# Long and short matmuls in turn: the two products of an MLP step, and the two parts of a token mix

## The chip, the cores and the metric

One core of a Trainium2 chip. The time is that of the device, in microseconds; the kernel before took 563.84 us in the median of three runs (562.71 to 564.00).

## The reference

Three stages on two batches of 768 tokens with 512 channels, all in fp32:

```
scores = q @ k.T / 8 - slope * distance;  keep: 96 positions back, and the first 8
x  = softmax(scores) @ v                                   # 8 heads of 64
xn = (x - mean(x)) / sqrt(var(x) + 1e-6) * g_ln
x  = x + relu(xn @ w_ch1) @ w_ch2                          # first mix: 512 -> 2048 -> 512
theta = x @ w_theta                                        # second mix
y  = W_r @ (x * cos(theta)) + W_i @ (x * sin(theta))       # token mix: 768 x 768, per batch
u  = x + y
out = u + relu(u @ w_ch)
```

## The kernel before

TensorE multiplies in fp32r, so every operand is split into a high and a low part, and every product is three matmuls: high x high, high x low, low x high.

**First mix.** The 12 tiles of 128 tokens are taken in 6 chunks of two tiles. The 2048 hidden channels are 16 blocks of 128, in four rounds of four blocks. A round has 24 steps, one for each chunk and block. A step computes, in `mlp_h`, the hidden block of a chunk, hp (128 hidden channels x 256 tokens): 12 matmuls of 256 columns (line 403). ScalarE takes the relu of it as hh (line 409), VectorE the rest as hl (line 410). In `mlp_o` hh and hl of an earlier step are the stationary operands and the rows of w_ch2 the moving ones: 6 matmuls of 512 columns into the two op tiles of the chunk (line 429). After the four blocks of a round op is scaled by the token's 1/std and added to x (`add_mix`, line 417).

What the names stand for: hh and hl are kept in three buffers each, in a pool where each buffer begins 64 bytes past a multiple of 512 in a partition's row. The banks of PSUM are handed out by tag: two "h" (hp), two "o", two "s", one "pt" and one "m". In rounds 2 and 3 every third hp goes to "m", so hp has three banks there, and in round 4 two.

**Order.** Round 1 runs beside the attention. The rounds 2 to 4 are the loop at lines 902 to 925: in each step first the 12 hp, then, where round 4's `early` has some, a piece of the second mix's start, then the 6 op of the step two before (of the step before, at the start of round 2 and in round 4), then the split of the weights that this freed (`split_w`, lines 362 to 372) and the decoding of the next ones (`decode`, lines 343 to 353; the weights arrive as packed words). A scheduler orders the instructions of each engine by their place in the program and their readiness in its own model; matmuls stand in the program's order but for small shifts.

**Second mix.** For each tile theta is 12 matmuls of 512 columns (thm, line 517); ScalarE and VectorE make cos and sin (`sincos`, lines 523 to 532) and the products with x (`rotate`, lines 536 and 537). The token mix (`tok`, line 606) takes one tile of 128 source tokens in a step, 12 steps in all, six for each batch: `tok_part` multiplies the channels of that tile (stationary) by the rows of W_r and W_i (moving). Part 0 gives target tokens 0 to 511 in four tiles of 512 columns, part 1 gives tokens 512 to 767 in four half tiles of 256; 24 matmuls each (line 582). They add up over a batch's six steps in six banks, taken as acc from the tags h, h, s, s, o, o; acc4 and acc5 hold part 1. In the batch's last step `add_y` (line 597) adds each acc to x on VectorE, and its bank is free. Behind it `last` multiplies by w_ch (ch, line 628) and writes the output.

```
banks = [ps(tag, [P, DM], f"acc{b}_{n}") for n, tag in enumerate(("h", "h", "s", "s", "o", "o"))]
for part in range(2):
    for d in range(KD):
        tok_part(b, s, d, part)
```

Of the kernel before, what the change touches and what calls it, by code (L numbers as in the profile page):

```python
# [1 line left out]

# [6 lines left out]
F32 = mybir.dt.float32  # L9
# [21 lines left out]
NE = 4  # L31
NPT = 2

PAD = 32


@with_exitstack
def kernel(ctx, tc, q, kwin, v, n_pair, g_ln, wall, out):
# [53 lines left out]
        nc.vector.scalar_tensor_tensor(nval, words[:, :, 1], 2.0**32, low, ALU.mult, ALU.add)  # L92

    def test_n():
        fast = act.tile([P, 6], F32, tag="bn", name="fast", bufs=2)
        nc.vector.tensor_scalar(fast[:, 0:1], nval[:, 0:1], 0.0, None, ALU.is_ge)
        nc.vector.tensor_scalar(fast[:, 1:2], nval[:, 0:1], float(GLOB), None, ALU.is_le)
        nc.vector.tensor_scalar(fast[:, 2:3], nval[:, 1:2], 1.0, None, ALU.is_ge)
        nc.vector.tensor_scalar(fast[:, 3:4], nval[:, 1:2], float(PREV), None, ALU.is_le)
        nc.vector.tensor_tensor(fast[:, 0:2], fast[:, 0:2], fast[:, 2:4], ALU.mult)  # L100
        nc.vector.tensor_tensor(fast[:, 0:1], fast[:, 0:1], fast[:, 1:2], ALU.mult)
        nc.vector.tensor_scalar(slow, fast[:, 0:1], -1.0, 1.0, ALU.mult, ALU.add)
# [252 lines left out]
    def decode_to(n):  # L355
        for i in range(len(piece), min(n, 2 * NF)):
            piece[i] = w_pool.tile([P, DM], F32, tag="w", name=f"w{i}", bufs=NW)
            decode(i, piece[i])
# [32 lines left out]
    def mlp_h(c, f, tag, part=None):  # L391
        cn = len(CHUNKS[c]) * P
        xh, xl = xt_t[c]
        wh, wl = split_t[f][0:2]
        if part != 1:
            hp_t[c, f] = ps(tag, [P, cn], f"hp{c}_{f}")
        hp = hp_t[c, f]
        kks = range(KD) if part is None else range(part * KD // 2, (part + 1) * KD // 2)
        n = 3 * kks[0]
        for kk in kks:  # L400
            a, al = wh[:, kk * P:(kk + 1) * P], wl[:, kk * P:(kk + 1) * P]
            for l, r in ((a, xh), (a, xl), (al, xh)):
                nc.tensor.matmul(hp, l, r[:, kk, :], start=(n == 0), stop=(n == 3 * KD - 1))  # L403
                n += 1
        if part == 0:
            return
        hh = act.tile([P, cn], F32R, tag="hh", name=f"hh{c}_{f}", bufs=3)
        hl = act.tile([P, cn], F32R, tag="hl", name=f"hl{c}_{f}", bufs=3)
        nc.scalar.activation(hh, hp, AF.Relu)  # L409
        nc.vector.scalar_tensor_tensor(hl, hp, 0.0, hh.bitcast(F32), ALU.max, ALU.subtract)  # L410
        ht_t[c, f] = (hh, hl)
# [7 lines left out]
    def mlp_o(c, f, fs, js=(0, 1)):  # L419
        if f == fs[0] and 0 in js:  # L420
            tags = ("s",) * 2 if c % 2 and f >= GROUP else ("o",) * 2
            op_t[c] = [ps(tags[j], [P, DM], f"op{c}_{f}_{t}") for j, t in enumerate(CHUNKS[c])]
        hh, hl = ht_t[c, f]
        wh, wl = split_t[f][2:4]
        for j in js:
            t = CHUNKS[c][j]
            a, al = hh[:, j * P:(j + 1) * P], hl[:, j * P:(j + 1) * P]
            for n, (l, r) in enumerate(((a, wh), (a, wl), (al, wh))):
                nc.tensor.matmul(op_t[c][j], l, r, start=(f == fs[0] and n == 0), stop=(f == fs[-1] and n == 2))  # L429
            if f == fs[-1]:  # L430
                add_mix(t, op_t[c][j])
                if f == NF - 1:
                    ready.add(t)

# [134 lines left out]
    def tok_part(b, s, d, part):  # L571

        w, z = toks[b, s], z_t[b * NQ + s]
        o = acc[b][part][d]
        dsl = slice(d * P, (d + 1) * P)
        for n, (zh, zl) in enumerate(z):
            wh, wl = w[1] if part else w[2 * n]
            sl = slice(n * SB, (n + 1) * SB) if part else slice(0, SA)
            for m, (l, r) in enumerate(((zh, wh), (zh, wl), (zl, wh))):
                first, end = s == 0 and n == 0 and m == 0, s == NQ - 1 and n == 1 and m == 2  # L580
                paired = part == 1
                mm = nc.tensor.matmul(  # L582
                    o, l[:, dsl], r[:, sl], start=first and not (paired and d % 2), stop=end and not (paired and d % 2 == 0)
                )
                if paired and (first or end):
                    tc.keep_in_program_order(mm)

    def x_cols(b, d, part):
        t0, t1 = (SA // P, NQ) if part else (0, SA // P)
# [16 lines left out]
    def tok(b, s):  # L606
        if s == 0:
            banks = [ps(tag, [P, DM], f"acc{b}_{n}") for n, tag in enumerate(("h", "h", "s", "s", "o", "o"))]
            acc[b] = (banks[0:KD], [banks[KD + d // 2][:, d % 2 * SB:(d % 2 + 1) * SB] for d in range(KD)])
        for part in range(2):  # L610
            for d in range(KD):
                tok_part(b, s, d, part)
                if s == NQ - 1:
                    for d_ in [d] if part == 0 else [d - 1, d] if d % 2 else []:
                        add_y(b, d_, part)
# [216 lines left out]

    def down(j, js):
        c, f = items[j]
        mlp_o(c, f, GROUPS[0], js)
        if js[-1] and c == NCH - 1 and f + GROUP < NF:
            split_w(f + GROUP)

# [2 lines left out]
    with tc.manual_schedule(engines=ENGINES):  # L841
        for k in range(LEAD + len(items) + 1):
            j = k - LEAD
            u = k - 1
            mix = 0 <= j < len(items)
            xp_of = HEAD + (k - 3) // U if k % U == 1 and 0 <= (k - 3) // U < NTT - HEAD else None
            xt_of = HEAD + (k - 4) // U if k % U == 0 and 0 <= (k - 4) // U < NTT - HEAD else None
            if k == 0:
                flip_probs(*blocks[1], 2, True)
                values(*blocks[1], 1)  # L850
                flip_probs(*blocks[1], 3, True)
                spin("o", "idle0", 5)
            if k == 1:
                values(*blocks[1], 2)
                values(*blocks[1], 3)
                lift_x(*blocks[1])
            if 0 <= u < NU:
                flip_probs(*unit(u)[:2], unit(u)[2][0], False)
            if k < NU:
                b, i, ps_ = unit(k)  # L860
                if k % U == 0:
                    loads_to(HEAD + k // U + 2)
                scores(b, i, ps_, False)
            if k == 1:
                make_xt(SEQ[0])
                finish_x(*blocks[1], True)
                layer_norm(SEQ[1])
            if k == 2:
                make_xt(SEQ[1])
            if mix:  # L870
                mlp_h(*items[j], "h", 0)
            elif 0 < k < LEAD:
                spin("o", f"idle{k}", 5)
            if 0 <= u < NU:
                flip_probs(*unit(u)[:2], unit(u)[2][1], False)
            if mix:
                mlp_h(*items[j], "h", 1)
            if xt_of is not None:
                make_xt(SEQ[xt_of])
            if 0 <= j - 1 < len(items):  # L880
                down(j - 1, [0])
            if xp_of is not None:
                finish_x(*blocks[xp_of], False)
            if 0 <= j - 1 < len(items):
                down(j - 1, [1])
            if 0 < k < LEAD:
                spin("o", f"wait{k}", 5)
            if 0 <= u < NU:
                for p in unit(u)[2]:
                    values(*unit(u)[:2], p)  # L890
                if u % U == U - 1:
                    lift_x(*unit(u)[:2])
            if xp_of is not None:
                layer_norm(SEQ[xp_of])
            if 0 <= k < 2 * GROUP - 2:
                with behind_exp(len(maxima) - 1):
                    split_w((k + 2) // 2, ((k + 2) % 2,))
            elif k >= 7:
                with behind_maximum(min(len(maxima) - 1, 16 + 4 * k + 3)):
                    decode_to(2 * GROUP + min(NW, (k - 5) // 2))  # L900
# [3 lines left out]
    for n, (g, c, f) in enumerate(work):  # L904
# [6 lines left out]
        if n == (NR - 2) * ROUND + 2 * NW + 1:  # L911
            early = early_steps()
        middle = ROUND + 2 <= n < (NR - 1) * ROUND
        mlp_h(c, f, "m" if middle and n % 3 == 0 else "h")
        next(early, None)
        while done[0] < n - (1 if middle else 0):
            pg, pc, pf = work[done[0]]
            mlp_o(pc, pf, GROUPS[pg])
            if pc == NCH - 1 and pf + GROUP < NF:
                split_w(pf + GROUP)  # L920
            done[0] += 1
        decode_to(2 * GROUP * (rnd + 1) + min(NW, n % ROUND // 2))
    for _ in early:
        pass
    mlp_o(*work[-1][1:], GROUPS[-1])

    act_es.close()
    ws_es.close()
# [90 lines left out]
```

## Time and profile before

| what | value |
|---|---|
| median of three runs | 563.84 us (562.71 to 564.00) |
| profiled execution | 563.2 us |
| its span | 561.4 us |
| TensorE busy | 546.8 us, 97% |
| VectorE, ScalarE, GpSimd busy | 359.8, 280.6, 103.4 us |
| share of PE in the chain that ended last | 66% |
| granted clock of TensorE, mean | 0.997 |

The span is the profiled stretch on the core; the execution's own time holds 1.8 us more around it. PE is TensorE's matmul, PEld its weight load, which overlaps it; DVE is VectorE, ACT ScalarE, POOL GpSimd. Matmuls follow one another in a pipeline, so the row of one shows a longer duration than the distance to the next one's start, and the distance is what it costs. [...]

### The profile page before, as it was taken

How to read it: one execution, taken by the hardware profiler on the slowest of the kernel's cores; microseconds unless marked ns; L12 is line 12 of the kernel's file. 1: busy time of each engine (PE TensorE's matmuls, PEld its weight loads, DVE VectorE, ACT ScalarE, POOL GpSimd, SP SyncE). 2: the span in 40 equal slices, each digit the busy share in tenths (PEclk: the TensorE clock that was granted, in tenths of full speed). 3: DMA queues.
4: the chain of work that ended last, by engine and by line, in shares of the span. 5: the costliest groups of instructions: out<-in, count | busy, mean ns of one | idle time of the engine just before them, and what ended most of it. 6: DMA issues, size and time to landing. Idle time of an engine off the chain costs nothing.

```text
span 561.4 us, 9278 instructions
## 1 busy us (share of the span) xinstructions
PE 546.8 (97%) x3554; PEld 461.9 (82%) x3557; DVE 359.8 (64%) x783; ACT 280.6 (50%) x647; POOL 103.4 (18%) x91
## 2 busy tenths in 40 slices
PE   8799999999998999999999999999999999999996
PEld 4367787787787999999889888889888888888895
DVE  6798787877757722298674424562699878870542
ACT  4677755555527411276562325561677777740110
POOL 1222100000013000030201102240033347730000
PEclk9999999999999999999999999999999999999998
DMA  8945544422013500045451000000234200000112
GB/s 260 338 157 188 195 148 142 133 76 74 13 67 112 188 1 1 0 151 189 149 188 39 0 1 1 0 2 2 104 122 147 78 2 0 2 1 1 75 72 85
DMA packets 18547, 49.17 MB, mean 88 GB/s; under 512 B 2240, under 2 KB 4288, under 8 KB 18496
## 3 DMA queue, kind: packets, MB, share of 16 engines
q1 hardware_dynamic: 18496, 48.51, 25.1%
q8 instruction: 30, 0.49, 0.3%
q14 instruction: 21, 0.17, 0.1%
HBM read 45.35 MB, written 3.15 MB: 86 GB/s over the span
## 4 chain that ended last, share of the span: by engine, by line
PE 66%; ACT 1%; DVE 1%; issue 0%; DVEq 0%; ACTq 0%
PE op L429 18%; PE hp L403 18%; PE acc L582 17%; PE thm L517 6%; PE ch L628 6%; PE xp L313 1%; DVE w L349 0%; ACT wt L343 0%; DVE hl L410 0%; ACT xth L314 0%; DVE dec L348 0%; ACT k L525 0%; ACT k L524 0%; ACT s L530 0%; ACT y L523 0%
## 5 line engine op out<-in xcount | busy, mean ns | idle before, releaser
L403 PE MATMUL hp<-xth,w1h 128*128 128x256 f32 x384 | 111.3, 290 | 0.0
L403 PE MATMUL hp<-xth,w1l 128*128 128x256 f32 x384 | 107.9, 281 | 0.0
L403 PE MATMUL hp<-xtl,w1h 128*128 128x256 f32 x384 | 107.8, 281 | 0.0
L410 DVE SCALAR_TENSOR_TENSOR hl<-hp,hh 128x256 fp32r<-128x256 f32 x96 | 40.3, 420 | 78.2 <-ACT hh L409 77.8
L403 PEld LDWEIGHTS hp<-xth,w1h 128*128 128x128 f32 x384 | 72.6, 189 | 9.2 <-issue 3.8
L582 PE MATMUL acc<-tokh,z 128*128 128x512 f32 (+1 forms) x320 | 79.2, 336 | 0.0
L429 PE MATMUL op<-w2h,hh 128*128 128x512 f32 x192 | 78.5, 409 | 0.0
L429 PE MATMUL op<-w2h,hl 128*128 128x512 f32 x192 | 76.4, 398 | 1.4 <-DVE hl L410 1.4
L429 PE MATMUL op<-w2l,hh 128*128 128x512 f32 x192 | 76.0, 396 | 0.0
L403 PEld LDWEIGHTS hp<-xtl,w1h 128*128 128x128 f32 x384 | 72.6, 189 | 3.7 <-DVE xtl L315 0.2
L409 ACT ACTIVATE hh<-hp 128x256 fp32r<-128x256 f32 x96 | 35.8, 374 | 74.4 <-PE hp L403 74.4
L403 PEld LDWEIGHTS hp<-xth,w1l 128*128 128x128 f32 x384 | 72.6, 189 | 0.1
L582 PEld LDWEIGHTS acc<-tokh,z 128*128 128x128 f32 x320 | 55.4, 190 | 6.6
L212 ACT ACTIVATE e<-e,nm 128x256 f32<-128x256 f32 (+1 forms) x96 | 46.0, 481 | 21.8 <-DVE nm L205 21.8
L582 PE MATMUL acc<-tokl,z 128*128 128x512 f32 (+1 forms) x160 | 53.8, 336 | 0.0
L371 POOL TENSOR_TENSOR w1l<-w,w1h 128x512 fp32r<-128x512 f32 x16 | 21.7, 1359 | 136.6 <-ACT w1h L370 136.6
L429 PEld LDWEIGHTS op<-w2h,hl 128*128 128x128 f32 x192 | 36.1, 188 | 12.6 <-DVE hl L410 4.0
L205 DVE CUSTOM_DVE_ANT_0 e<-s,bias 128x256 f32<-128x256 f32 (+1 forms) x96 | 33.5, 397 | 16.8 <-PE s L231 16.7
L544 POOL TENSOR_TENSOR x2all<-xth,xtl 128x512 f32<-128x512 f32 x12 | 18.3, 1527 | 121.1 <-DVE k L536 121.1
L494 DVE TENSOR_TENSOR tokl<-wt,tokh 128x512 fp32r<-128x512 f32 x36 | 34.0, 952 | 10.3 <-ACT tokh L493 10.1
L429 PEld LDWEIGHTS op<-w2h,hh 128*128 128x128 f32 x192 | 36.4, 190 | 4.3 <-ACT hh L409 0.4
L429 PEld LDWEIGHTS op<-w2l,hh 128*128 128x128 f32 x192 | 36.2, 188 | 3.8
(155 smaller groups left out, 1055.0 us busy)
## 6 DMA issues: line engine op xcount, KB each, us to landing
raw<-in_wall SPq DMA_DIRECT2D x58, 512.0 KB, 3.2
k<-in_kwin SPq DMA_DIRECT2D x10, 512.0 KB, 4.8
q<-in_q SPq DMA_DIRECT2D x12, 256.0 KB, 3.5
vc<-in_v SPq DMA_DIRECT2D x12, 256.0 KB, 3.4
out<-o SPq DMA_DIRECT2D x8, 256.0 KB, 2.0
vw<-in_v SPq DMA_DIRECT2D x10, 192.0 KB, 2.5
out<-o SPq DMA_DIRECT2D x8, 128.0 KB, 1.7
vw<-in_v SPq DMA_DIRECT2D x10, 64.0 KB, 3.6
```

Of the source, the lines that this page charges most:

```text
L205: r = nc.vector.tensor_tensor_reduce(out=e[:, j, :], in0=s[j], in1=bias[h][:, b0:b0 + nk], scale=-SCALE, scalar=3.0e38, op0=ALU.add, op1=A ...
L212: r = nc.scalar.activation(e[:, j, :], e[:, j, :], AF.Exp, bias=nm[:, h:h + 1], scale=-1.0, accum_out=sm[:, h:h + 1])
L371: (nc.vector if d and f >= GROUP else nc.gpsimd).tensor_tensor(lo, s, hi.bitcast(F32), ALU.subtract)
L403: nc.tensor.matmul(hp, l, r[:, kk, :], start=(n == 0), stop=(n == 3 * KD - 1))
L409: nc.scalar.activation(hh, hp, AF.Relu)
L410: nc.vector.scalar_tensor_tensor(hl, hp, 0.0, hh.bitcast(F32), ALU.max, ALU.subtract)
L429: nc.tensor.matmul(op_t[c][j], l, r, start=(f == fs[0] and n == 0), stop=(f == fs[-1] and n == 2))
L494: nc.vector.tensor_tensor(lo, src, hi.bitcast(F32), ALU.subtract)
L517: nc.tensor.matmul(mp, l[:, kk, :], r[:, kk, :], start=(n == 0), stop=(n == 3 * KD - 1))
L544: nc.gpsimd.tensor_tensor(x2[t], xh.rearrange("p k t -> p (k t)").bitcast(F32), xl.rearrange("p k t -> p (k t)").bitcast(F32), ALU.add)
L582: mm = nc.tensor.matmul(o, l[:, dsl], r[:, sl], start=first and not (paired and d % 2), stop=end and not (paired and d % 2 == 0))
L628: nc.tensor.matmul(mp, l[:, kk, es], r, start=(kk == 0 and m == 0), stop=(kk == KD - 1 and m == 2))
```

## The change

In rounds 2 to 4 `mlp_h` and `mlp_o` become generators, and a new function `run` draws from several of them in turn: two hp matmuls, one op matmul, six times a step. The op now belong to the step three before (two before in round 4), and the piece of `early` and the split of weights stand behind both. hh and hl have four buffers in place of three, and begin at multiples of 512 bytes, for which a small tile `fast` goes to another pool and a filler (PAD) shrinks from 32 to 24 words. In the token mix, in all but the last step of each batch, the matmuls of part 0 and part 1 alternate one by one. The number of matmuls, loads and vector instructions is the same. The added lines shift line numbers by 2 to 17: op stands at 432, hp at 405, hh and hl at 412 and 413, thm at 533, acc at 598, the add to x at 614.

```diff
-PAD = 32
+LAG = 3
+PAD = 24
...
-        fast = act.tile([P, 6], F32, tag="bn", name="fast", bufs=2)
+        fast = keep.tile([P, 6], F32, name="fast")
...
                 nc.tensor.matmul(hp, l, r[:, kk, :], start=(n == 0), stop=(n == 3 * KD - 1))
                 n += 1
+                yield
...
-        hh = act.tile([P, cn], F32R, tag="hh", name=f"hh{c}_{f}", bufs=3)
-        hl = act.tile([P, cn], F32R, tag="hl", name=f"hl{c}_{f}", bufs=3)
+        hh = act.tile([P, cn], F32R, tag="hh", name=f"hh{c}_{f}", bufs=4)
+        hl = act.tile([P, cn], F32R, tag="hl", name=f"hl{c}_{f}", bufs=4)
...
+    def run(*gens):
+
+        live = list(gens)
+        while live:
+            for g, n in list(live):
+                for _ in range(n):
+                    if next(g, live) is live:
+                        live.remove((g, n))
+                        break
...
+        if s < NQ - 1:
+            for d in range(KD):
+                run(*((tok_part(b, s, d, part), 1) for part in range(2)))
+            return
         for part in range(2):
             for d in range(KD):
-                tok_part(b, s, d, part)
+                run((tok_part(b, s, d, part), 1))
...
-        mlp_h(c, f, "m" if middle and n % 3 == 0 else "h")
+        steps = [(mlp_h(c, f, "m" if middle and n % 3 == 0 else "h"), 2)]
+        behind_ = []
+        while done[0] <= n - (LAG if n < (NR - 1) * ROUND else 2):
+            behind_.append(work[done[0]])
+            done[0] += 1
+        if behind_:
+            steps.append((chain(*(mlp_o(*x[1:], GROUPS[x[0]]) for x in behind_)), len(behind_)))
+        run(*steps)
         next(early, None)
-        while done[0] < n - (1 if middle else 0):
-            pg, pc, pf = work[done[0]]
-            mlp_o(pc, pf, GROUPS[pg])
-            if pc == NCH - 1 and pf + GROUP < NF:
-                split_w(pf + GROUP)
-            done[0] += 1
+        for x in behind_:
+            if x[1] == NCH - 1 and x[2] + GROUP < NF:
+                split_w(x[2] + GROUP)
```

On PE, in the first steps of round 2, the kernel before has the last hp of chunk 0, block 7, then the 6 op of block 5, then the hp of chunk 1 (the first numbers in a name are the chunk and the block):

```order
L403 MATMUL hp0_7_2411<-xtl0_480,w1h7_2331 128x256
L403 MATMUL hp0_7_2411<-xth0_479,w1l7_2332 128x256
L429 MATMUL op0_4_0_2378<-w2h5_2288,hh0_5_2374 128x512 [waits Activation_49]
L429 MATMUL op0_4_0_2378<-w2l5_2289,hh0_5_2374 128x512
L429 MATMUL op0_4_0_2378<-w2h5_2288,hl0_5_2375 128x512 [waits DVE_49]
L429 MATMUL op0_4_6_2379<-w2h5_2288,hh0_5_2374 128x512
L429 MATMUL op0_4_6_2379<-w2l5_2289,hh0_5_2374 128x512
L429 MATMUL op0_4_6_2379<-w2h5_2288,hl0_5_2375 128x512
L403 MATMUL hp1_4_2434<-xth1_768,w1h4_2253 128x256
L403 MATMUL hp1_4_2434<-xtl1_769,w1h4_2253 128x256
```

The same engine and place in the changed kernel, where the op of block 5 stand among the hp of chunk 1:

```order
L432 MATMUL op0_4_6_2407<-w2h4_2257,hl0_4_2358 128x512
L405 MATMUL hp1_4_2428<-xth1_768,w1h4_2253 128x256 [waits DVE_49]
L405 MATMUL hp1_4_2428<-xtl1_769,w1h4_2253 128x256
L432 MATMUL op0_4_0_2406<-w2h5_2288,hh0_5_2374 128x512 [waits Activation_49]
L405 MATMUL hp1_4_2428<-xth1_768,w1l4_2254 128x256
L405 MATMUL hp1_4_2428<-xth1_768,w1h4_2253 128x256
L432 MATMUL op0_4_0_2406<-w2l5_2289,hh0_5_2374 128x512
L405 MATMUL hp1_4_2428<-xtl1_769,w1h4_2253 128x256
L405 MATMUL hp1_4_2428<-xth1_768,w1l4_2254 128x256
L432 MATMUL op0_4_0_2406<-w2h5_2288,hl0_5_2375 128x512
```

The op have moved one step later, and the wait on VectorE now stands at the first hp of a step, for its bank.

On PE, at the first token-mix step of the second batch, the kernel before ends part 0 (acc1_3) before it begins part 1 (acc1_4):

```order
L582 MATMUL acc1_3_5394<-tokh1_0_0_5199,z0_6_4897 128x512 [waits DVE_49]
L582 MATMUL acc1_3_5394<-tokl1_0_0_5200,z0_6_4897 128x512
L582 MATMUL acc1_3_5394<-tokh1_0_0_5199,z0_6_4897 128x512
L582 MATMUL acc1_3_5394<-tokh1_0_2_5207,z1_6_4900 128x512
L582 MATMUL acc1_3_5394<-tokl1_0_2_5208,z1_6_4900 128x512
L582 MATMUL acc1_3_5394<-tokh1_0_2_5207,z1_6_4900 128x512
L582 MATMUL acc1_4_5395<-tokh1_0_1_5203,z0_6_4897 128x256 [waits DVE_49,PE_49]
L582 MATMUL acc1_4_5395<-tokl1_0_1_5204,z0_6_4897 128x256
```

In the changed kernel the same step begins, behind the last thm of tile 10, with:

```order
L533 MATMUL thm10_5357<-thh_3490,xtl10_5212 128x512
L598 MATMUL acc1_0_5391<-tokh1_0_0_5199,z0_6_4897 128x512 [waits DVE_49]
L598 MATMUL acc1_4_5395<-tokh1_0_1_5203,z0_6_4897 128x256 [waits DVE_49,PE_49]
L598 MATMUL acc1_0_5391<-tokl1_0_0_5200,z0_6_4897 128x512
L598 MATMUL acc1_4_5395<-tokl1_0_1_5204,z0_6_4897 128x256
L598 MATMUL acc1_0_5391<-tokh1_0_0_5199,z0_6_4897 128x512 [waits Pool_49]
L598 MATMUL acc1_4_5395<-tokh1_0_1_5203,z0_6_4897 128x256
```

The first matmul into acc1_4, with its wait on VectorE, has moved from the step's 25th place to its second. VectorE's own order there, which frees acc0_4, is the same in both kernels:

```order
L614 TENSOR_TENSOR x2all_70<-x2all_70,acc0_3_4670 128x4x128 [waits PE_49]
L614 TENSOR_TENSOR x2all_70<-x2all_70,acc0_4_4671 128x2x128 [waits PE_49]
L552 SCALAR_TENSOR_TENSOR k9_5233<-k9_5233,x2all_70 128x512 [waits Activation_49]
L614 TENSOR_TENSOR x2all_70<-x2all_70,acc0_4_4671 128x2x128
L614 TENSOR_TENSOR x2all_70<-x2all_70,acc0_5_4672 128x2x128 [waits PE_49]
L614 TENSOR_TENSOR x2all_70<-x2all_70,acc0_5_4672 128x2x128
```

Between the two halves of acc0_4 stands k, a product of the rotation of tile 9; nothing has moved.

## Rows read from the trace of the kernel before

**Rows 1.** The page: busy time by engine, and the chain's shares by line.
```profile
PE 546.8 (97%) x3554; PEld 461.9 (82%) x3557; DVE 359.8 (64%) x783; ACT 280.6 (50%) x647; POOL 103.4 (18%) x91
...
PE op L429 18%; PE hp L403 18%; PE acc L582 17%; PE thm L517 6%; PE ch L628 6%; PE xp L313 1%; DVE w L349 0%; ACT wt L343 0%; DVE hl L410 0%; ACT xth L314 0%; DVE dec L348 0%; ACT k L525 0%; ACT k L524 0%; ACT s L530 0%; ACT y L523 0%
```
**Rows 2.** The chain in order of time: start us, us, what.
```profile
180.15 2.87 PE hp L403 x24
...
208.43 1.42 PE hp L403 x12
209.85 1.40 PE op L429 x6
...
273.29 1.42 PE hp L403 x12
...
280.66 1.55 PE op L429 x6
...
337.84 1.42 PE hp L403 x12
...
444.70 2.75 PE thm L517 x12
447.45 8.31 PE acc L582 x48
```
**Rows 3.** PE's timeline behind a run of 256 columns: start us, us, what.
```profile
489.90 0.40 PE L582 MATMUL acc<-tokl,z 128*128 128x512 f32 x1
...
490.60 0.39 PE L582 MATMUL acc<-tokl,z 128*128 128x512 f32 x1
...
491.28 0.39 PE L582 MATMUL acc<-tokl,z 128*128 128x512 f32 x1
```
**Rows 4.** PE's timeline in the second batch's first token-mix step.
```profile
470.29 0.39 PE L582 MATMUL acc<-tokh,z 128*128 128x512 f32 x1
470.52 0.39 PE L582 MATMUL acc<-tokl,z 128*128 128x512 f32 x1
...
475.85 0.28 PE L582 MATMUL acc<-tokl,z 128*128 128x256 f32 x1
...
478.61 0.40 PE L517 MATMUL thm<-thh,xth 128*128 128x512 f32 x1
```
**Rows 5.** PE's timeline where the two sizes mix in round 4.
```profile
356.50 0.40 PE L517 MATMUL thm<-thl,xth 128*128 128x512 f32 x1
356.74 0.28 PE L403 MATMUL hp<-xth,w1l 128*128 128x256 f32 x1
356.85 0.28 PE L403 MATMUL hp<-xth,w1h 128*128 128x256 f32 x1
...
357.09 0.42 PE L517 MATMUL thm<-thh,xtl 128*128 128x512 f32 x1
```
**Rows 6.** VectorE's timeline beside the step of rows 4.
```profile
471.04 1.01 DVE L597 TENSOR_TENSOR x2all<-x2all,acc 128x512 f32<-128x512 f32 x2
471.99 1.38 DVE L536 SCALAR_TENSOR_TENSOR k<-k,x2all 128x512 f32<-128x512 f32 x1
473.29 1.07 DVE L597 TENSOR_TENSOR x2all<-x2all,acc 128x256 f32<-128x256 f32 x3
```
**Rows 7.** VectorE's timeline: hl at three places.
```profile
182.76 0.41 DVE L410 SCALAR_TENSOR_TENSOR hl<-hp,hh 128x256 fp32r<-128x256 f32 x1
...
280.54 0.42 DVE L410 SCALAR_TENSOR_TENSOR hl<-hp,hh 128x256 fp32r<-128x256 f32 x1
...
341.90 0.42 DVE L410 SCALAR_TENSOR_TENSOR hl<-hp,hh 128x256 fp32r<-128x256 f32 x1
```
**Rows 8.** Stretches at the end: us, busy by engine, granted clock, DMA share, GB/s.
```profile
556.50:558.50 2.00, 0.00 (x0) 0.00 (x0) 0.42 (x1) 0.00 (x0) 0.00 (x0) 1.00 0.35 118
558.50:559.50 1.00, 0.00 (x0) 0.00 (x0) 0.00 (x0) 0.00 (x0) 0.00 (x0) 0.54 0.09 25
```
**Rows 9.** PE's timeline at the program's start.
```profile
1.19 4.94 PE L77 MATMUL spin<-zero 128*128 128x512 bf16 x12 [1.19 <-DVE zero L119]
```

More of the change, by code (lines that the diff above doesn't have):

```diff
@@ L1 @@
 from contextlib import ExitStack
+from itertools import chain
 import concourse.bass as bass
@@ L429, in mlp_o @@
                 nc.tensor.matmul(op_t[c][j], l, r, start=(f == fs[0] and n == 0), stop=(f == fs[-1] and n == 2))
+                if n < 2:
+                    yield
             if f == fs[-1]:
@@ L433, in mlp_o @@
                     ready.add(t)
+            yield
+    def run(*gens):
[6 more added lines that the diff above has]
+                        break
     p2 = {}
@@ L586, in tok_part @@
                     tc.keep_in_program_order(mm)
+                yield
     def x_cols(b, d, part):
@@ L834, in down @@
         c, f = items[j]
-        mlp_o(c, f, GROUPS[0], js)
+        run((mlp_o(c, f, GROUPS[0], js), 1))
         if js[-1] and c == NCH - 1 and f + GROUP < NF:
@@ L870 @@
             if mix:
-                mlp_h(*items[j], "h", 0)
+                run((mlp_h(*items[j], "h", 0), 1))
             elif 0 < k < LEAD:
@@ L876 @@
             if mix:
-                mlp_h(*items[j], "h", 1)
+                run((mlp_h(*items[j], "h", 1), 1))
             if xt_of is not None:
@@ L913 @@
         middle = ROUND + 2 <= n < (NR - 1) * ROUND
-        mlp_h(c, f, "m" if middle and n % 3 == 0 else "h")
-        next(early, None)
-        while done[0] < n - (1 if middle else 0):
-            pg, pc, pf = work[done[0]]
-            mlp_o(pc, pf, GROUPS[pg])
-            if pc == NCH - 1 and pf + GROUP < NF:
-                split_w(pf + GROUP)
-            done[0] += 1
+        steps = [(mlp_h(c, f, "m" if middle and n % 3 == 0 else "h"), 2)]
[6 more added lines that the diff above has]
+        run(*steps)
+        next(early, None)
+        for x in behind_:
+            if x[1] == NCH - 1 and x[2] + GROUP < NF:
+                split_w(x[2] + GROUP)
         decode_to(2 * GROUP * (rnd + 1) + min(NW, n % ROUND // 2))
+    run((mlp_o(*work[-2][1:], GROUPS[-1]), 1))
     for _ in early:
         pass
-    mlp_o(*work[-1][1:], GROUPS[-1])
+    run((mlp_o(*work[-1][1:], GROUPS[-1]), 1))
     act_es.close()
```

## The prediction

> **What bounds the kernel now.** I began with the busy shares and the chain that ended last [rows 1]: TensorE is busy 97% of the 561.4 us span, VectorE 64%, ScalarE 50%, and the chain runs through PE for two thirds of the span, mostly through three lines, op and hp of the first mix and acc of the token mix. The reader should see that the other engines only matter where PE waits for them. Then I read the chain in order of time [rows 2]. A step of rounds 2 to 4 is 12 hp matmuls in 1.42 us and 6 op matmuls in 1.40 us, 2.82 us; a token-mix step is 48 matmuls in 8.31 us. With no wait between, what can change is the time of one matmul and the waits at the edges. So the third view was PE's timeline, where the distance between starts is the cost of one matmul in its place (its own duration also holds the fill of the pipeline).
>
> Four prices come from it. An op costs 1.40/6 = 233 ns, an hp 1.42/12 = 118 ns. The 512-column matmuls of the second mix are cheaper: 2.75/12 = 229 for thm, and for acc 227, namely 490.60 to 491.28 is 0.68 us for three [rows 2, 3]; 23 matmuls of 256 columns take 475.85 to 478.61, 120 each [rows 4]. What tells op from acc is where the stationary operand begins, 64 bytes past a multiple of 512 for hh and hl, on such a multiple for the rest. I take the 6.5 ns for the price of that.
>
> **The interleaving of the first mix.** No matmul is added or removed: 69 of the 72 steps of rounds 2 to 4 now issue hp, hp, op six times (in the first three there is no op to lay between). Such a triple costs 2 x 118 + 233 = 470 ns before. The trace of before has few places where the sizes mix. Behind a run of 256 columns the first three 512s come at 0.70/3 = 233 (489.90 to 490.60) and later ones at 227 [rows 3]. At 356.50 a thm, three hp and a thm stand in turn: 0.24 us to the first hp, then 0.35 for the three, 117 each [rows 5]. So an aligned op behind an hp may cost 227 or 235, and hp 113 (the shortest that any switch shows by itself, about 0.11 between 356.74 and its next) to 120. The bounds of a triple are 226.5 + 2 x 113 = 452.5 and 236 + 2 x 120 = 476 ns; six triples and 69 steps make that 69 x 6 x (452.5 - 470) = -7.2 us and +2.5 us. The places seen lie in the middle, (227 + 235)/2 + 113 + 120 = 464: I take 464, 69 x 6 x -6 ns = **-2.5 us**.
>
> The op of round 1 (24 steps x 6) become aligned too, but PE waits for the attention's other engines in most of that round; where it does not (some ten steps), 60 x 6.5 ns = **-0.4 us**, between 0 and -0.9.
>
> **The interleaving of the token mix.** In 10 of the 12 steps a 512 and a 256 stand in turn, 24 of each. Before they cost 24 x (227 + 120) = 8.31 us [rows 2, 4]. In turn each 512 is behind a 256 (235) and each 256 behind a 512 (113): 24 x 348 = 8.35. That is nothing, **0 us**, with 10 x 24 x (226.5 + 113 - 347) = -1.8 us as the low end and 10 x 24 x (236 + 120 - 347) = +2.2 us as the high end.
>
> **A wait that is new.** In the first step of the second batch, acc1_4 takes the bank that acc0_4 held, and VectorE has to add acc0_4 to x first. Before, 24 matmuls of the first part stand ahead of it: the step begins at 470.29, acc1_4 at about 475.73, just before the 475.85 [rows 4]. Now acc1_4 is the step's second matmul, at 470.52. VectorE's order there is the same as before. It adds the first half of acc0_4 by 472.05, then does the k of the rotation for 1.38 us, and the second half is the first of the three at 473.29, ended about 0.41 later [rows 6]. So PE stands from 470.52 to about 473.7, **+3.2 us** (2.5 to 3.5). Queued behind it on PE is the rest of the step, which has nothing else to run, and as PE finds all it needs later in time, nothing gives the wait back. Other banks that change hands earlier (acc0_4 after the first mix, acc0_2 in bank s) have been free for microseconds.
>
> **The lag of three steps.** In round 3 VectorE, which decodes weights there, is late with hl: that of the hp at 273.29 ends at 280.96, 7.7 us after the step began, and an op piece of 1.55 instead of 1.40 us shows a wait of PE, one of four such between 276 and 291 us, about 0.6 us together [rows 2, 7]. Now op uses hl 3 x 2.78 + 1.2 = 9.5 us after its step began, but the hp three steps on needs the bank that hl frees, at 8.3 us. If VectorE's times hold, that is later than before by 0.8 us and the waits go, -0.6; but hp now ends a microsecond later in its step, and hl starts behind it, which could cost 1 us once. I take **0** (-0.6 to +1.0). The buffers that hold hh and hl, four instead of three, are what this needs.
>
> In round 4 hp has only two banks, so hl must be there 2.78 + 0.24 = 3.0 us after its hp ended; the latest in the trace is 341.90 + 0.42 against an hp that ended at 339.26, 3.06 us [rows 2, 7]: **+0.2 us** (0 to 0.8). At the start of round 2 three hp groups now follow one another with no op between, and the third needs the hl that ends at 183.17, when hp stands ready at 183.02 [rows 2, 7]: **+0.2 us** (0 to 0.4). The move of `fast` out of a pool changes an address only; VectorE's, ScalarE's and the DMA queues' orders move by a place or two, w2 of a step is split one step later, and no PE wait shows behind it: 0.
>
> **Sum.** -2.5 - 0.4 + 0 + 3.2 + 0 + 0.2 + 0.2 = +0.7 us on the profiled execution of 563.2 us (span 561.4 and 1.8 around it), so 563.9; the median of the runs, 563.84, lies 0.6 above that execution, so I predict 564.5 us.
>
> **Rivals.**
> (B) The turn of short and long hides what is lost between matmuls: the triple falls to its low end, 452.5 ns. For it speaks the first 256 behind a 512, at 113 instead of 120; against it that the 512 behind a 256 is dearer by the same. It gives 563.84 - 7.2 - 0.4 + 3.6 = 559.8 us, and 558.0 if the token mix gains its 1.8 too.
> (C) Neither order nor alignment counts: op stays at 233 because of something else that tells it from acc. Then only the waits stay, 563.84 + 3.6 = 567.4 us. Against it: thm and acc, with the same shapes, at 229 and 227 [rows 2, 3]. [...]
> (D) The end on the other side: the new wait lets TensorE's clock fall. After the last matmul, 556.5, the granted clock was 1.00 until 558.5 and 0.54 on the mean of the next microsecond [rows 8], so an idle time of about 2 us was enough there, and the new wait is 3.2. How long the half clock lasts after work begins again is not in the trace; the first 12 matmuls of the program, after a start at rest, took 4.94 us where 12 x 0.227 = 2.7 us would be full speed [rows 9], so up to 2.2 us are lost. It decides as soon as the wait is over about 2 us. With 2.0 us the time is 566.5 us. Against it: the fall at the end came behind work that had thinned out to nothing, while here 12 matmuls of thm stand ahead of the wait and 47 of acc behind it.
> (E) The wait is short or missing, since VectorE gets to acc0_4 earlier when PE is: then 564.5 - 3.2 = 561.3 us. Against it: VectorE's order is fixed, and it was never ahead there.
>
> **How the numbers follow.** A measurement of this kernel can tell about 0.3%, 1.7 us: faster is below 562.15, slower above 565.5. The forecast has 0.33 (its own range 562.5 to 566.5: same 0.22, slower 0.09, faster 0.02); B 0.22, faster; C 0.16, slower; D 0.20, slower but for 0.03; E 0.09, faster 0.06 and same 0.03. That makes faster 0.30, same 0.28, slower 0.42. The range that leaves 2 in 10 out goes from B, 559.8, to a little over D and C, 568.5 (both together would be 569.4).
>
> **What would show it.** In the profile after: a step of round 2 should take 2.78 us in the chain, with op at 231 ns or less; 2.72 is B, 2.82 C. A token step should keep 8.3 to 8.4 us. One idle time on PE of 2.5 to 3.5 us at the first acc of the second batch, with VectorE's add to x named as its releaser, and the granted clock of the following microseconds, decide D and E. A waiting time of PE on hl above 1 us in round 3 would prove the lag's zero wrong. The forecast as a whole is wrong if a step moves by more than 0.1 us either way.

## The result, and the profile after

The changed kernel took 571.26 us in the median of five runs (570.12 to 572.42) against 564.0 (562.71 to 565.29): ratio 1.013, 95% interval 1.0115 to 1.0146, slower by 7.3 us. The forecast was 564.5. The profiled execution is one of 571.98 us, with a span of 570.2.

Busy time on the page after, and the clock in 40 slices, which answer to [rows 1]:

```profile
PE 551.0 (97%) x3557; PEld 464.3 (81%) x3557; DVE 360.6 (63%) x783; ACT 280.9 (49%) x647; POOL 103.1 (18%) x91
...
PEclk9999999999999999999999999999999997999999
```

PE has 4.2 us more busy time for the same matmuls (three records of them are missing before), the span is 8.8 us longer, and one slice of the clock stands at 7 and not at 9. The chain in order of time, answering to [rows 2] (start, us, what):

```profile
205.40 0.23 PE op L432
...
208.20 0.23 PE op L432
...
211.00 0.23 PE op L432
...
447.70 8.47 PE acc L598 x48
...
461.92 3.37 DVE tokl L510 x3
...
473.39 1.29 DVE k L552
474.68 0.34 DVE x2all L614
475.15 10.88 PE acc L598 x47
486.03 2.75 PE thm L533 x12
```

The same op of three steps stands 2.80 us apart: a step of the first mix is 0.02 us shorter than the 1.42 + 1.40 of before, not 0.04. A token-mix step in turn is 8.47, not 8.31. And before the second batch's first step the chain leaves PE for VectorE. PE's timeline there (start, us, what, idle time before it and who ended it), answering to [rows 4], and its granted clock by stretches (us, then PE, PEld, DVE, ACT, POOL busy, clock, DMA share, GB/s):

```profile
470.52 0.39 PE L533 MATMUL thm<-thh,xtl 128*128 128x512 f32 x1
470.74 0.39 PE L598 MATMUL acc<-tokh,z 128*128 128x512 f32 x1
475.15 0.55 PE L598 MATMUL acc<-tokh,z 128*128 128x256 f32 x1 [4.02 <-DVE x2all L614]
475.50 0.84 PE L598 MATMUL acc<-tokl,z 128*128 128x512 f32 x2
```

```profile
470.90:475.10 4.20, 0.23 (x2) 0.00 (x0) 4.04 (x8) 3.62 (x7) 2.25 (x2) 0.85 0.00 0
475.10:476.00 0.90, 0.85 (x3) 0.78 (x4) 0.90 (x3) 0.90 (x3) 0.90 (x2) 0.50 0.00 0
...
479.00:480.00 1.00, 1.00 (x5) 0.81 (x5) 0.90 (x3) 0.86 (x2) 1.00 (x1) 0.50 0.00 0
480.00:481.00 1.00, 1.00 (x5) 0.85 (x5) 0.99 (x1) 0.00 (x0) 1.00 (x2) 0.65 0.00 0
481.00:482.00 1.00, 1.00 (x8) 0.87 (x7) 0.97 (x1) 0.00 (x0) 1.00 (x2) 1.00 0.02 8
```

The reader should see three things in one place: the second matmul of the step waits 4.02 us for the add to x; the mean clock is already below 1 in that idle time; and the matmuls that follow run at 0.50 until some point between 480 and 481. VectorE beside it, answering to [rows 6]:

```profile
472.38 1.01 DVE L614 TENSOR_TENSOR x2all<-x2all,acc 128x512 f32<-128x512 f32 x2
473.33 1.35 DVE L552 SCALAR_TENSOR_TENSOR k<-k,x2all 128x512 f32<-128x512 f32 x1
474.60 1.07 DVE L614 TENSOR_TENSOR x2all<-x2all,acc 128x256 f32<-128x256 f32 x3
```

The same three rows in the same order, 1.3 us later than before, while PE is only 0.45 later.

The books, from the distances between starts in the two profiles. By the end of the first mix the changed kernel is ahead by 0.3 us (0.55 if counted from the first step of round 2, where it was 0.26 behind). The wait then costs 4.2 (4.41 to the next start, of which 0.24 is the matmul). The slow clock costs 2.5: the step lasts 15.13 us, less the wait and less a step in turn of 8.47. Nine of the ten steps in turn cost 1.4 together (the first, which waits in any case, nothing), and thm 0.1. In all the last matmul ends 7.8 us later. The other microsecond of the span lies behind it, in the last output's transfer, and the medians don't show it.

### The profile page after: what moved, and what is told of

It is laid out like the page before. It is cut to its first block, busy times and chain, and to the rows that moved or that the text cites. A ratio compares the mean times of both kernels' runs of the same rounds, so it can differ in the third digit from the quotient of the medians.

```text
span 570.2 us, 9275 instructions
## 1 busy us (share of the span) xinstructions
PE 551.0 (97%) x3557; PEld 464.3 (81%) x3557; DVE 360.6 (63%) x783; ACT 280.9 (49%) x647; POOL 103.1 (18%) x91
## 4 chain that ended last, share of the span: by engine, by line
PE 63%; DVE 4%; ACT 1%; issue 0%; ACTq 0%; DVEq 0%
PE op L432 17%; PE acc L598 17%; PE hp L405 17%; PE ch L649 6%; PE thm L533 6%; PE xp L315 1%; DVE tokl L510 1%; DVE x2all L614 1%; DVE w L351 0%; DVE y L543 0%; DVE dec L350 0%; DVE w2l L373 0%; DVE y L544 0%; DVE y L542 0%; DVE k L552 0%
## 5 line engine op out<-in xcount | busy, mean ns | idle before, releaser
L598 PE MATMUL acc<-tokh,z 128*128 128x512 f32 (+1 forms) x320 | 74.6, 346 | 4.0 <-DVE x2all L614 4.0
L432 PE MATMUL op<-w2h,hh 128*128 128x512 f32 x192 | 77.3, 403 | 0.0
L598 PEld LDWEIGHTS acc<-tokh,z 128*128 128x128 f32 x320 | 52.2, 194 | 12.1 <-issue 4.4
L510 DVE TENSOR_TENSOR tokl<-wt,tokh 128x512 fp32r<-128x512 f32 x36 | 36.1, 1023 | 16.7 <-ACT tokh L509 16.5
L420 DVE SCALAR_TENSOR_TENSOR x2all<-op,rsall,x2all 128x512 f32<-128x512 f32 x48 | 35.5, 746 | 16.2 <-PE op L432 16.2
L598 PE MATMUL acc<-tokl,z 128*128 128x512 f32 (+1 forms) x160 | 44.5, 344 | 0.0
```

Source lines behind the costliest of these rows:

```text
L420: nc.vector.scalar_tensor_tensor(x2[t], o, rsall[:, t:t + 1], x2[t], ALU.mult, ALU.add)
L510: nc.vector.tensor_tensor(lo, src, hi.bitcast(F32), ALU.subtract)
L598: mm = nc.tensor.matmul(o, l[:, dsl], r[:, sl], start=first and not (paired and d % 2), stop=end and not (paired and d % 2 == 0))
```

## The experiments

The comparisons with before are ratios with their 95% intervals; experiments of one group share their runs of before. Theory after the result: all of the loss is in the token mix, as wait, fallen clock and dearer matmuls. The rivals stand in the expectations.

**Where the loss is.** First mix as changed, token mix as before:

```diff
-        if s < NQ - 1:
+        if False:
             for d in range(KD):
                 run(*((tok_part(b, s, d, part), 1) for part in range(2)))
```

> The first mix as in the changed kernel, the token mix as before (part 0, then part 1). Theory: the whole loss is in the token mix (a wait of 4.0 us at the second batch, 2.6 us of half clock behind it, 10 steps x 0.16 us of dearer matmuls); the first mix gained 0.5 us in the profile. So 563.5 us (563.0 to 564.2), no idle time of PE above 0.3 us at the second batch, granted clock 0.997, an acc step of 8.31 us. Rival: the new lag and banks of the first mix take part in the loss; then the time stays above 565.5 us.

Measured: 563.11 us, ratio 0.9986 (0.9977 to 0.9994). Acc steps of 8.31, no idle time at the second batch, clock 0.998; the batch's first step in the chain (start, us, what):

```profile
470.32 8.31 PE acc L598 x48
```

The first mix's change by itself is a small gain of 0.6 us. And the other half alone, the kernel before with the token mix in turn (the new branch of `tok`, `run` and the `yield` in `tok_part`, nothing else):

> The kernel before with the token mix in turn in ten steps, the first mix as before. Theory: all of the loss is here: wait 4.0, half clock 2.6, 10 x 0.16: 563.9 + 8.2 = 572 us (571.3 to 572.8), clock 0.993. Rival: part of the wait comes from the first mix's new order (VectorE later at the second batch): 570 us or less.

Measured: 572.19 us, ratio 1.0141 (1.0125 to 1.0158): the wait is 3.4 us, the clock again at half behind it. The wait's total (us, times, longest) and one stretch behind it:

```profile
PE acc L594 <- DVE x2all L610: 3.4, 1, 3.4
```

```profile
477.00:478.00 1.00, 1.00 (x4) 0.87 (x4) 0.22 (x1) 1.00 (x5) 1.00 (x1) 0.50 0.00 0
```

The loss is the token mix's. The wait is 0.6 us shorter than in the changed kernel: against before, PE begins the step 1.9 us later here (0.45 there), and VectorE reaches its adds 2.2 us later (1.3 there). So the last 0.6 us came only with both changes together, as the rival had it in part; why, these runs don't show.

**Wait and clock apart.** 16 matmuls that nobody needs fill the wait:

```diff
             acc[b] = (banks[0:KD], [banks[KD + d // 2][:, d % 2 * SB:(d % 2 + 1) * SB] for d in range(KD)])
+            if b == 1:
+                for _ in range(16):
+                    nc.tensor.matmul(banks[0], mats["th"][0][:, 0, 0:P], mats["th"][0][:, 0, :], start=True, stop=True)
```

> The changed kernel, and ahead of the first token-mix step of the second batch 16 matmuls of 512 columns that nobody needs (their bank is started anew behind them), 16 x 0.23 = 3.7 us: PE reaches the waiting matmul as late as VectorE frees the bank. Theory: the wait is VectorE's and stays in another form, 3.7 of work and 0.3 of waiting, but PE isn't idle and the granted clock stays 1.00: 571.3 - 2.6 = 568.7 us (568.0 to 569.3). Rival: the slow stretch behind the wait has another cause than idleness (VectorE's or ScalarE's pace there); then 571 us and again about 5 us at a granted clock of 0.5.

Measured: 568.44 us, ratio 1.0079 (1.0066 to 1.0093); 2.8 us less than the changed kernel with more work on PE. Its PE timeline, and the stretches behind:

```profile
470.77 3.79 PE L629 MATMUL acc<-thh 128*128 128x512 f32 x16
474.40 0.39 PE L598 MATMUL acc<-tokh,z 128*128 128x512 f32 x1
475.22 0.36 PE L598 MATMUL acc<-tokh,z 128*128 128x256 f32 x1 [0.43 <-DVE x2all L614]
```

```profile
475.30:477.00 1.70, 1.70 (x10) 1.52 (x11) 1.14 (x3) 1.70 (x6) 1.70 (x2) 1.00 0.00 0
477.00:480.00 3.00, 3.00 (x18) 2.58 (x18) 2.29 (x2) 2.91 (x6) 3.00 (x3) 1.00 0.00 0
```

PE reaches the bank at the same moment, 475.2, and goes on at 1.00. Behind the wait the chain has the same 47 matmuls in 8.49 us that took 10.88 in the changed kernel:

```profile
475.22 8.49 PE acc L598 x47
```

The fallen clock is a consequence of the idle time, and costs 2.4 to 2.8 us of its own. What happens without the wait is the other half:

```diff
-        if s < NQ - 1:
+        if s < NQ - 1 and (b, s) != (1, 0):
```

> The changed kernel, but the first token-mix step of the second batch issues part 0 and then part 1, as before; the other nine steps alternate. Theory: wait and fallen clock go together: 571.3 - 4.0 - 2.6 = 564.7 us (564.0 to 565.3), with acc steps of 8.47 us still. Rival 1: the clock falls because of the alternation and not of the idle time: 567.3 us, clock at 0.5 in some other stretch. Rival 2: the wait only moves to the next bank that VectorE is late with: above 567 us.

Measured: 567.44 us, ratio 1.0062 (1.0043 to 1.008). Wait and half clock are gone, but only 3.8 us came back of the 6.6 expected: rival 2 in another form. The waits of PE name a new one:

```profile
PE acc L598 <- DVE tokl L510: 1.5, 2, 0.9
```

It stands in the batch's fourth step (1.1 us more than a matmul at 499.98, 0.7 at 502.07); a thm ahead of the second step waits 0.5 us besides. VectorE makes tokl from tokh, and ScalarE's timeline shows where tokh comes from, here and, in the second fence, in the kernel before:

```profile
495.13 0.63 ACT L546 ACTIVATE s<-y 128x512 f32<-128x512 f32 x1 [3.39 <-DVE y L544]
...
496.85 0.61 ACT L509 ACTIVATE tokh<-wt 128x512 fp32r<-128x512 f32 x1
497.70 0.63 ACT L564 ACTIVATE z<-k 128x512 fp32r<-128x512 f32 x1 [0.24 <-DVE k L552]
498.24 0.62 ACT L564 ACTIVATE z<-s 128x512 fp32r<-128x512 f32 x1
498.76 2.69 ACT L509 ACTIVATE tokh<-wt 128x512 fp32r<-128x512 f32 x5
```

```profile
490.11 1.14 ACT L493 ACTIVATE tokh<-wt 128x512 fp32r<-128x512 f32 x2
...
497.23 1.66 ACT L493 ACTIVATE tokh<-wt 128x512 fp32r<-128x512 f32 x3
```

Before, two of the three blocks of the fourth step are made at 490, in a pause of ScalarE. The buffers of the second step, which they take, are free by then, since part 0 has read two of the three blocks after half a step. In turn all three are read to the step's end, and the scheduler puts two of them behind the products of tile 11. It is the order that makes them late, and not ScalarE's load: the second step ends at 491.15 here, and ScalarE stands idle for 3.39 us before 495.13. A test: the second step put back as well (the edit is shown against the kernel just named).

```diff
-        if s < NQ - 1 and (b, s) != (1, 0):
+        if s < NQ - 1 and (b, s) not in ((1, 0), (1, 1)):
```

> The changed kernel, but the first two token-mix steps of the second batch issue part 0 and then part 1; the other eight steps in turn. Theory: the 2.2 us that PE waited for tokl in the fourth step of the second batch, when only the first was put back, come from the second step: in turn it reads all three blocks of token weights to its end, their buffers come free 2.9 us later, and ScalarE makes two of the three blocks for the fourth step behind the products of tile 11 and not ahead of them. With the second step put back, ScalarE's order there is that of the kernel before: no wait for tokl, 563.1 + 8 x 0.16 = 564.4 us (564.0 to 565.0). Rival: VectorE is late there whatever the order, since PE has no idle time to give it: the waits stay and the time is 566.5 us or more.

Measured: 564.81 us, ratio 1.0014 (1.0004 to 1.0024), and no wait for tokl. ScalarE's row is back in its place:

```profile
491.20 1.14 ACT L509 ACTIVATE tokh<-wt 128x512 fp32r<-128x512 f32 x2
```

So the turn has a third price, the later release of buffers, after which the scheduler makes their next contents in a later place; the changed kernel has no wait for tokl, and its long wait at the batch's start is the likely reason. More buffers for these blocks would test it more directly; that wasn't tried.

**The bank.** Another order of banks in the second batch:

```diff
-            banks = [ps(tag, [P, DM], f"acc{b}_{n}") for n, tag in enumerate(("h", "h", "s", "s", "o", "o"))]
+            banks = [ps(tag, [P, DM], f"acc{b}_{n}") for n, tag in enumerate(("s", "s", "o", "o", "h", "h") if b else ("h", "h", "s", "s", "o", "o"))]
...
-            last(1, e, part, ("m", "pt", "h", "s")[k_ % 4])
+            last(1, e, part, ("m", "pt", "s", "o")[k_ % 4])
```

> The changed kernel, but the second batch takes its banks in another order, s, s, o, o for part 0 and h, h for part 1 (and the last products of w_ch take m, pt, s, o in turn), so that acc1_4 gets the bank that VectorE frees first. Theory: the wait of 4.0 us is for that one bank; it falls below 0.5 us with VectorE's work the same, and the clock stays; the price in turn (1.6 us) remains, and tokl comes late behind, as in the kernel without the turn in that step (2 to 2.7 us): 567 to 568 us. Rival: VectorE is late with every bank by then, and a wait of 3 us stays: 570 us or more.

Measured: 568.32 us, ratio 1.0075 (1.006 to 1.0091). The wait at the second batch shrinks to half a microsecond (the step lasts 8.98, of which 8.47 are matmuls in turn): it was for that one bank. The rest is above the expectation for a reason that it did not foresee. PE's timeline at the wait for tokl, and the clock behind it:

```profile
501.05 0.38 PE L598 MATMUL acc<-tokl,z 128*128 128x256 f32 x1 [1.22 <-DVE tokl L510]
501.27 0.86 PE L598 MATMUL acc<-tokh,z 128*128 128x512 f32 x4
502.75 0.62 PE L598 MATMUL acc<-tokl,z 128*128 128x512 f32 x2 [0.61 <-DVE tokl L510]
```

```profile
503.00:504.00 1.00, 1.00 (x5) 0.84 (x5) 1.00 (x3) 0.00 (x0) 0.00 (x0) 0.68 0.00 0
504.00:505.00 1.00, 1.00 (x4) 0.81 (x4) 0.50 (x1) 0.00 (x0) 0.00 (x0) 0.50 0.00 0
```

Two waits of 1.2 and 0.6 us with five matmuls between them brought the clock down as well, to 0.50 until some point between 506 and 507. The kernel without the turn in the second batch's first step had the same two waits, 0.9 and about 0.6, and kept 1.00:

```profile
503.00:504.00 1.00, 1.00 (x5) 0.88 (x6) 1.00 (x2) 0.00 (x0) 0.00 (x0) 1.00 0.00 0
```

Each of these is one execution. In the runs without a trace the two kernels may differ less: with the other order of banks, two of four have a mean clock of 0.992 and take 568.8 and 569.2 us (the profiled one is the latter), two have 0.997 and 0.998 and take 567.9 and 567.4; of the six without the turn in that step, one has 0.991 and 569.2 us, the others 0.997 or 0.998 and 567.8 at most. That the clock fell in some executions of either kernel and not in others fits this, but isn't shown: the mean clock of the kernel before varies from 0.991 to 1.000 with no such difference in time.

**The price of the turn.** In the first batch alone:

```diff
-        if s < NQ - 1:
+        if s < NQ - 1 and b == 0:
```

> The changed kernel with the token mix in turn in the first batch only (five steps). Theory: a step in turn costs 0.16 us more, so 563.11 + 5 x 0.16 = 563.9 us; no wait at the second batch, granted clock 0.997. Whether VectorE's tokl, late at 499.98 and 502.07 us of the kernel whose second batch began with part 0 and went on in turn (2.2 us of waits), is late here too: the theory says no, since part 1 is needed 24 matmuls later again; the rival (VectorE's order was changed by the first batch too) says a wait of 2 us there, 566 us.

Measured: 564.35 us, ratio 1.001 (1.0001 to 1.0019), no wait behind; its steps take 8.47 us by the distances between starts, so 4 x 0.16, and the first, which waits in any case, nothing. The median is 1.2 us above the 563.11 with no step in turn, and about half of that is left unexplained. And turns of six, one tile each:

```diff
-                run(*((tok_part(b, s, d, part), 1) for part in range(2)))
+                run(*((tok_part(b, s, d, part), 6) for part in range(2)))
```

(with the second batch's first step as before)

> The changed kernel with part 0 and part 1 of the token mix in turns of six (a tile of part 0, then a half tile of part 1), and the second batch's first step as before. Read in the steps of the first batch. If the extra 6.3 ns of a pair is paid at every change of length, a step has 8 changes in place of 48 and costs 8.31 + 0.16 / 6 = 8.34 us; if it is paid for the same weights being used twice in a row (part 0 and part 1 of one product follow each other with the same stationary block), it goes altogether: 8.31 us; if it goes with the share of long and short alone: 8.47 us.

Measured in a single run: 565.76 us, steps of 8.374 us in the first batch. That is none of the three: 0.06 us dearer than in blocks of 24. In these steps the first five 512s behind a 256 come at 233, 236, 228, 233 and 231 ns, the sixth at 226, and the first 256 behind a 512 at 114, later ones at 119 and 120. So a round of 6 + 6 that begins behind a 256 takes 2.10 us, 0.02 more than at the prices of steady rows, and three of a step's four rounds do. What sets the price of a change stays open. In the second batch these turns, too, wait once for tokl, 1.2 us. Behind it 92 matmuls take 16.14 us; two steps of 8.374 less four of their 96 matmuls would be 16.05, so they keep their pace.

**The first mix.** hh and hl moved to multiples of 512 bytes in the kernel before:

```diff
-PAD = 32
+PAD = 24
...
-        fast = act.tile([P, 6], F32, tag="bn", name="fast", bufs=2)
+        fast = keep.tile([P, 6], F32, name="fast")
```

> The kernel before, and only hh and hl begin at multiples of 512 bytes (three buffers as before; the small tile moved and the filler shrunk as in the change). Theory: in steps of 12 + 6 the alignment gives the op 18 ns and takes them back from the hp behind, 2.820 us either way (round 1 of the changed kernel shows it); only op x12 in a row gain, 0.08 us: 563.8 us, ratio within 0.1% of 1. Rival (the prediction's reading of 227 and 233 ns): 576 x 6.5 ns less where PE is busy, 561 us.

Measured: 563.73 us, ratio 1.0001 (0.9992 to 1.001). The chain in order of time:

```profile
311.20 1.43 PE hp L403 x12
312.64 1.39 PE op L429 x6
314.02 1.43 PE hp L403 x12
315.46 2.75 PE op L429 x12
```

The op gain 0.01 us in a step and the hp lose it. Only where 12 op stand in a row do they reach 2.75/12 = 229 ns; before, such a row took 2.80/12 = 233 to 234 each:

```profile
314.87 2.80 PE op L429 x12
```

And the reverse, the first mix in turn with hh and hl 64 bytes off (PAD and `fast` as before, token mix as before):

> First mix in turn with lag 3 and four buffers, token mix as before, but hh and hl begin 64 bytes past a multiple of 512 again. Theory: aligned, a triple in turn costs 466.7 ns, and a block of 12 + 6 costs 2.820 us aligned or not; so alignment is worth little or nothing and the step keeps 2.80 us: 563.1 us, as with the first mix alone in turn (563.11). Rival: the turn pays only with aligned tiles; a triple of 470 to 476 ns, 69 x 6 x (3.3 to 9) ns = 1.4 to 3.9 us more, 564.5 to 567 us.

Measured: 563.22 us, ratio 0.9991 (0.9982 to 1.0), steps of 2.80 us up to the last round: like 563.11 with them aligned. The alignment is worth nothing that shows here.

A lag of two steps:

```diff
-LAG = 3
+LAG = 2
```

(token mix as before)

> First mix in turn, token mix as before, op two steps behind its hp in rounds 2 and 3 instead of three. Theory: the waits of round 3 (about 0.8 us, gone in the changed kernel) come from the op's need of hl two steps on; with the lag of two, op needs hl at 2 x 2.80 + 1.2 = 6.8 us after its step began, VectorE is 7.7 late: 0.9 us or more are lost, 564.0 to 564.8 us against 563.11. Rival: the bank of hp, not the op, sets the waits, and they stay away: 563.1 us.

Measured: 565.67 us, ratio 1.0031 (1.0019 to 1.0043), 2.6 us more than with three. The longest waits in round 3, and the totals of that wait for the whole run:

```profile
275.11 0.50 PE L432 MATMUL op<-w2h,hl 128*128 128x512 f32 x1 [0.22 <-DVE hl L413]
...
279.61 0.50 PE L432 MATMUL op<-w2h,hl 128*128 128x512 f32 x1 [1.43 <-DVE hl L413]
```

```profile
PE op L432 <- DVE hl L413: 3.1, 4, 1.4
```

With three steps it is 1.4 us, all of it between 176 and 180 us, ahead of round 2. The four steps of round 3 around the longest wait last 2.8 us more than 4 x 2.80, which is the whole loss. The op's need of hl sets the waits of round 3, and the third step of lag is what the turn needs.

**A faster version.** Round 4 in blocks, as before:

```diff
-        run(*steps)
-        next(early, None)
+        if n < (NR - 1) * ROUND:
+            run(*steps)
+            next(early, None)
+        else:
+            run(steps[0])
+            next(early, None)
+            run(*steps[1:])
```

(with the op one step behind in round 4, and the token mix as before)

> First mix in turn in rounds 2 and 3 with lag 3; in round 4 hp, then early, then op one step behind, as before; token mix as before. Theory: the profile of the changed kernel gained 1.2 us on before by the end of round 3 and gave back 0.8 in round 4, where pieces of the second mix stand behind the op; that is kept here, 563.1 - 0.8 = 562.3 us. Rival: round 4 gives it back anyway (its op of three steps come in a row at the start): 563.1 us.

Measured: 562.26 us, ratio 0.9971 (0.9959 to 0.9983): faster than both kernels, by 1.6 us than before.

## Why the prediction was wrong

The direction was forecast as undecided with slower the likeliest (0.42), and slower it was, but the time lies 6.8 us above the forecast and 2.8 above the range. The largest single miss is the clock. Without its 2.5 us the time would still be 568.8, a little above the range, so the smaller misses, nearly all of them upward, had their part. Step by step:

- **The clock (rival D).** This is the step that failed: the sum put the clock at nothing behind a wait of 3.2 us that it had itself. The prediction had a row that speaks for the fall [rows 8] and one for the price [rows 9], and yet gave it 0.20. The half clock lasted over five microseconds behind the wait and cost 2.5, a little over the 2.2 named as its upper end. A wait of 3.2 us and "the clock may fall" were not two cases but one: the matmuls on either side, which spoke against it, did not keep the clock up, which was at 0.50 before the wait was over. The "about 2 us" of idle time was one row's; the fall behind waits of 1.2 and 0.6 us, with the other order of banks, shows that it is no lower bound.
- **The wait** was found, in its place and with its releaser, and sized 3.2; it was 4.0 idle, 4.2 on the chain. The missing part is VectorE 1.3 us later against PE's 0.45. The order of VectorE at the place was indeed the same; what came ahead of it was not: the three tokl of 461.92 now wait for ScalarE, which makes their tokh behind the two products z, and run in one piece. "Orders move by a place or two" and "no PE wait shows behind it: 0" passed over this, and with it over the buffers that the turn frees later.
- **The token mix in turn** was 0 (-1.8 to +2.2) and is +1.4. 235 + 113 = 348 ns per pair was read from single changes of length; in a turn one by one the pair costs 353. By the distances between starts the 512s come there at 232, 241 and 236 ns and the 256s at 118, 120 and 113, three pairs over and over: only every third 256 is as short as the one that was read.
- **The first mix in turn** was -2.5 and is -0.02 x 69 = -1.4; a triple costs 467 ns, between the forecast's 464 and the 470 of before. Round 3's waits went, as the low end of that term had it (-0.6; measured -0.7). Round 4 gave back 0.7: the ten steps around the pieces of the second mix last 1.0 us longer than before, the others 0.02 less each, so it is not the banks that the +0.2 was for; in blocks, as in the faster version, round 4 keeps the gain. What delays these steps in turn was not followed up. The start of round 2 cost 0.4 where 0.2 was forecast: its third group of hp stands still behind its first matmul, and these two take 0.62 us in place of 0.24:

```profile
183.10 0.78 PE L405 MATMUL hp<-xth,w1h 128*128 128x256 f32 x2
183.72 0.28 PE L405 MATMUL hp<-xtl,w1h 128*128 128x256 f32 x1
```

- **The alignment** was -0.4 in round 1 and a share of the triple; it is 0. The difference of 227 and 233 ns is mostly the place behind a run of 256 columns, and only beyond five or six op in a row the tile's start. So rival C was right that the alignment counts for nothing with op in blocks of six. The order did count, by -1.4 us in the first mix and +1.4 in the token mix, and C's sum of 567.4 lacks the clock. The loads for hp, op and acc last 188 to 194 ns in the mean in either profile; they overlap one another there (3557 loads in 464 us busy), so what one costs is not shown.

## What to carry to other kernels

When a reordering puts the first use of a shared buffer or bank ahead, look up in the trace when its last reader ends; the distance is a wait. A wait of TensorE of some microseconds is to be priced with the slow clock behind it, in the sum and not among the rivals: here 4 us of waiting brought 2.5 more. Turning two streams into one also lengthens the life of what both read, and the scheduler may then put the making of the next contents behind other work, even where the engine has a pause earlier (here ScalarE's of 3.39 us). Prices of single changes in the trace didn't add up to the price of a regular turn here (348 ns a pair against 353); measure the pattern by itself.

## What the runs showed of the hardware

- Waits of 1.2 and 0.6 us with five matmuls between them brought TensorE's clock down to 0.50 in one traced run; behind waits of 0.9 and about 0.6 in another it stayed at 1.00, and behind one of 1.2 in a third 92 matmuls kept their pace (16.14 us, 16.05 by the steps of the first batch).
- Sixteen matmuls whose result nobody needs, laid into a wait of 4 us, kept the clock at 1.00 and made the kernel 2.8 us faster; the 47 matmuls behind the wait took 8.49 us in place of 10.88.
- In steady rows a matmul of 256 columns cost 120 ns and one of 512 columns 227, so 107 for 256 columns more. At these prices a step of the first mix is 12 x 120 + 6 x 227 = 2.80 us; it cost 20 ns more in blocks, aligned or not (2.82 us), and nothing more in turn, two hp and one op (2.80); one 512 and one 256 in turn cost 6 ns a pair more (353 against 347).
